# One PSUM ring of four banks in place of two pairs, and attention ahead of the weights in the prologue

## The chip, the cores and the metric

One core of one Trainium2 chip runs the program. The metric is device time in microseconds (us). Three timed runs of the kernel before took 955.02 to 955.73 us, median 955.3.

## The reference

```python
scores = (q @ k.T) / sqrt(64)                  # 4 batches, 8 heads, 576 positions, head size 64
# heads 0-3: window of 32 positions; heads 4-7: 32 positions with dilation 4
attn = softmax(where(mask, scores, -1e9)); x = attn @ v        # -> 2304 tokens x 512
h = x @ w_in;  x = (s * relu(h)**2 + b) @ w_out                # 512 -> 2048 -> 512
h = x @ w_in2; out = (h * cos(h)) @ w_out2                     # 512 -> 2048 -> 512
```

## The kernel before

The tokens are cut into five tiles of 384, 384, 512, 512 and 512 columns (tiles 0 to 4). For both MLPs (m = 0, 1) and each tile there are 16 steps, one per slice of 128 hidden rows. Step p of the program multiplies slice p into a PSUM tile `h` (`mm_in`), and multiplies the activated slice of two steps earlier into four PSUM tiles `y` (`mm_out`). From tile 1 on each product is three fp32r matmuls (high and low parts); tile 0 of the first MLP uses plain fp32 matmuls.

Attention is cut into units: 192 positions of a pair of heads. A unit is a matmul for the scores (`a_scores`, tile `sc`), a softmax on VectorE (mask and scale into `sm`, maximum) and ScalarE (the exponentials, three or four instructions), a normalisation on VectorE (`a_norm`), a transpose on TensorE (`a_transpose`, tile `tp`) with a copy into `pt`, a product with v (`a_pv`, tile `pv`) and a copy into the input `xy` of the MLP. Units 0 to 7 make tile 0 and run in the prologue, k = 0 to 11: iteration k issues scores of unit k, normalisation of unit k-1, transpose of unit k-3 and pv of unit k-4. The later units run beside the first MLP, one tile of tokens ahead: a unit whose scores stand in step p has its softmax at the end of p, its normalisation at the head of p+1, its transpose at the end of p+2 and its pv in p+4. In steps 15 to 26 and 31 to 42 there is a unit in every step; they are called dense here. A softmax buffer `sm` is one of two, so the softmax of a unit waits until the transpose of the unit before last has read its buffer.

The weights come as 64-bit words, 32 halves of 128x512 per MLP (half 2f feeds `mm_in` of slice f, half 2f+1 feeds `mm_out`). A half is loaded on SP's queue (`w_load`, 512 KB), opened by two ScalarE instructions (`w_float`) and joined by four VectorE instructions (`w_join`); `w_whole(n)` joins up to half n and opens one half further. `W_FIRST` says behind which attention loads the first four halves are loaded, `W_STEPS` after which prologue iterations how many halves are joined, and `w_point` joins up to half 2p + WPRE (rounded with the half step) in step p of tile 0.

Engines take their instructions in the order in which they are written; the schedule is by hand. PSUM has eight banks: four for y, two for h (`ps_h`), two for sc, tp and pv (`ps_a`). A pool hands out its banks in turn, so in a pool of two a tile waits until the tile before last has been read. In the second MLP h alternates between the two pools.

Of the kernel before, what the change touches and what calls it, by code (L numbers as in the profile page):

```python
# [28 lines left out]
NCC = DM // P  # L29
NFC = DFF // P  # L30
LAG = (2, 3)
W_FIRST, W_STEPS = (3, 5, 6, 7), {5: 1, 7: 2, 8: 3, 9: 4, 10: 5, 11: 6}
V_LATE = 3
AHEAD = 3
WPRE, W_PACE = 7, 2.0
IN_CUT = 13

BG = (0, 4, 8, 10, 10)
# [14 lines left out]
def attention_then_two_mlps(ctx, tc, qk_p, qk_d, v_p, v_d, mask_p, mask_d, w1, w2, sv, bv, out):  # L53
    nc = tc.nc
    pool = lambda name, bufs, **kw: ctx.enter_context(tc.tile_pool(name=name, bufs=bufs, **kw))
    PSUM = bass.MemoryType.PSUM
# [4 lines left out]
    xspool = pool("xs", 4)  # L61
    gpool = pool("g", 1)
    ps_y = pool("ps_y", 1, space=PSUM)
    ps_h = pool("ps_h", 2, space=PSUM)
    ps_a = pool("ps_a", 2, space=PSUM)

    s_sb = const.tile([P, 1], F32, tag="s_sb", name="s_sb")
    b_sb = const.tile([P, 1], F32, tag="b_sb", name="b_sb")
# [107 lines left out]
    def a_load_first(i, what):  # L176
        tb, hp = units[i]
        b, u = divmod(tb, 3)
        dil = hp >= 2
        nb, nq, nk = (4, DB, DK) if dil else (3, PB, PK)  # L180
        kw = nb * nk if dil else 3 * PB + WINDOW
        d = st.setdefault(i, dict(dil=dil, nb=nb, nq=nq, nk=nk, tb=tb, hp=hp, b=b, u=u))
        place = lambda n, shape: wpool.tile(
            shape, F32, tag=("wh", "wl")[(5 * i + n) % 2] + str(2 * NFC - 1 - (5 * i + n) // 2), name=f"first{n}_{i}"
        )
        d["place"] = place
        if what == "v":
            d["v"] = place(2, [nk, nb, P])
            nc.sync.dma_start(d["v"], (v_d if dil else v_p)[b, hp % 2, u])
        else:  # L190
            src = (qk_d if dil else qk_p)[b, hp % 2, u]
            d["q"], d["k"] = place(0, [P, 384]), place(1, [P, kw])
            nc.sync.dma_start(d["q"], src[:, :384])
            nc.sync.dma_start(d["k"], src[:, 384:])
# [60 lines left out]
    def a_norm(i):  # L255
        d = st[i]
        nb, nq, nk = d["nb"], d["nq"], d["nk"]
        nr = 2 * nq
        rec = ap_.tile([nr, nb, 1], F32, tag="rec", name=f"rec{i}")
        nc.vector.tensor_scalar_add(d["ssum"], d["ssum"], 1e-9)  # L260
        nc.vector.reciprocal(out=rec[:, :, 0], in_=d["ssum"])
        nc.vector.tensor_tensor(out=d["sm"], in0=d["sm"], in1=rec.to_broadcast([nr, nb, nk]), op=ALU.mult)

    def a_transpose(i, ps, copy=None):
        d = st[i]
        nb, nq, nk = d["nb"], d["nq"], d["nk"]
        nr = 2 * nq
        acc = ps.tile([P, 512], F32, tag=ps_tag[ps.name], name=f"tp{i}")
        for j in range(nb):
            nc.tensor.transpose(acc[:nk, j * nr : (j + 1) * nr], d["sm"][:, j, :], ident[:nr, :nr])  # L270
        pt = d["place"](4, [nk, 384]) if "place" in d else ap_.tile([nk, 384], F32, tag="pt", name=f"pt{i}")
        (copy or nc.vector.tensor_copy)(pt, acc[:nk, :384])
        d["pt"] = pt
# [25 lines left out]
                src = acc[:, lo:hi]  # L299
            nc.scalar.copy(dst, src)  # L300

    ps_tag = {ps_y.name: "y0", ps_h.name: "h", ps_a.name: "a"}


    xs = {}
# [12 lines left out]
    def mm_in(m, t, fc, ps):  # L318
        h = ps.tile([P, 512], F32, tag=ps_tag[ps.name], name=f"h{m}_{t}_{fc}")
        hps[m, t, fc] = h  # L320
        for cc in range(NCC):
            cs = slice(cc * P, (cc + 1) * P)
            if m == 0 and t == 0:
                w = w32[m, 2 * fc].bitcast(F32)
                nc.tensor.matmul(  # L325
                    h[:, : SIZES[t]], w[:, cs], xy[t][:, cc, :], start=cc == 0, stop=cc == NCC - 1
                )
                continue
            x = xs[m, t, cc]
            hi, lo = wh[m, 2 * fc][:, cs], wl[m, 2 * fc][:, cs]  # L330
            nc.tensor.matmul(h[:, : SIZES[t]], hi, x[:, 0, :], start=cc == 0, stop=False)  # L331
            nc.tensor.matmul(h[:, : SIZES[t]], hi, x[:, 1, :], start=False, stop=False)  # L332
            nc.tensor.matmul(h[:, : SIZES[t]], lo, x[:, 0, :], start=False, stop=cc == NCC - 1)  # L333
# [96 lines left out]
    with tc.manual_schedule():  # L430
# [4 lines left out]
        def w_load_to(n):  # L435
            while wq[0] < min(n, 2 * NFC):
                w_load(0, wq[0], stage.tile([P, DM], I64, tag=f"s{wq[0] % 5}", name=f"stage{wq[0]}"))
                wq[0] += 1
# [18 lines left out]
        for i in range(1, n0 + V_LATE):  # L457
            if i < n0:
                a_load_first(i, "qk")
            if 0 <= i - V_LATE < n0:  # L460
                a_load_first(i - V_LATE, "v")
            if i == 3:
                nc.sync.dma_start(m_d, mask_d.rearrange("p (j k) -> p j k", j=2))
            if i == 5:
                nc.sync.dma_start(s_sb, sv.to_broadcast([P, 1]))
                nc.sync.dma_start(b_sb, bv.to_broadcast([P, 1]))
            if i in W_FIRST:
                w_load_to(wq[0] + 1)
        a_load(n0)
        a_load(n0 + 1)  # L470
        for k in range(n0 + 4):
            if k < n0:
                a_scores(k, ps_a)
                a_softmax(k)
            if 0 <= k - 1 < n0:
                a_norm(k - 1)
            if 0 <= k - 3 < n0:
                a_transpose(k - 3, ps_h, nc.scalar.copy if k % 2 else None)
            if 0 <= k - 4 < n0:
                a_pv(k - 4, ps_y, f"y{k % NCC}")  # L480
            if k in W_STEPS:
                w_whole(W_STEPS[k])
# [7 lines left out]
        for i in range(n0, len(units)):  # L490
            t = next(t for t in range(NTILE) if i < first_unit[t + 1])
            n, j = first_unit[t + 1] - first_unit[t], i - first_unit[t]
            p = (t - 1) * NFC + ((0, 1, 3, 4, 6, 8, 9, 10)[j] if n == 8 else j - 1)
            at((p, 0), lambda i=i: a_scores(i, ps_a))
            at((p + 1, 1), lambda i=i: a_load_v(i))
            if i + 2 < len(units):
                at((p, 0), lambda i=i: a_load(i + 2))
            at((p, 1), lambda i=i: a_softmax(i))
            at((p + 1, 0), lambda i=i: a_norm(i))
            at((p + 2, 2), lambda i=i: a_transpose(i, ps_a, nc.scalar.copy))  # L500
            at((p + 4, 0), lambda i=i: a_pv(i, ps_a))
# [16 lines left out]
        k = 0  # L518
        for t, n in enumerate(BG):
            for i in range(n):  # L520
                b = t * NFC + (2 if t == 1 else 0) + (i + 0.5) * (NFC - (2 if t == 1 else 0)) / n
                p, ph = int(b), 1 + int(b % 1 >= 0.5)
# [17 lines left out]
        for p in range(NP + LAG[1]):  # L540
            if p < NP:
                m, t, fc = where(p)
                mm_in(m, t, fc, ps_h if (m == 0 or fc % 2 == 0) else ps_a)
                nxt = p - fc + NFC
                if nxt < NP:
                    mm, tt, _ = where(nxt)
                    for cc in {NFC - 1: range(NCC)}.get(fc, ()):
                        x_split(mm, tt, cc)
            fire(p, 0)
            if p < NP and m == 1:  # L550
                cos1(t, fc)
            if NTILE * NFC <= p - 1 < NP:
                cos_split(*where(p - 1)[1:])
            po = p - LAG[0] if p < NTILE * NFC + LAG[0] else p - LAG[1]
            out_now = po >= 0 and p != NTILE * NFC + LAG[0]
            last = out_now and where(po)[2] == NFC - 1
            if last:
                mm_out(*where(po))
                y_out(*where(po)[:2])
            if p < NP:  # L560
                w_point(p, 0)
                if m == 0:
                    relu2(t, fc)
                else:
                    cos2(t, fc)
                    cos3(t, fc)
            if out_now and not last:
                mm_out(*where(po))
            if p < NFC * NTILE:
                w_point(p, 1)  # L570
            f = p - NFC * (NTILE - 1)
            if 0 <= f < NFC:
                w_fetch(2 * f)
            if 0 <= f - LAG[0] < NFC:
                w_fetch(2 * (f - LAG[0]) + 1)
            fire(p, 1)
            fire(p, 2)
            if p == NFC:
                assert wq[2] == 2 * NFC
                stage_scope.close()  # L580
                late.append(ctx.enter_context(tc.tile_pool(name="late", bufs=1, side="right", reuse_waits="tile")))
            if p == NFC * (NTILE - 1) - 1:
                att.close()
                after_att.append(ctx.enter_context(tc.tile_pool(name="after_att", bufs=1)))
                for t in (0, 1):
                    xy[t] = after_att[0].tile([P, NCC, SIZES[t]], F32, tag=f"xy{t}", name=f"back{t}")
                    nc.sync.dma_start(xy[t], parked[t])
# [88 lines left out]
```

## Time and profile before

| | us |
|---|---|
| median of three runs | 955.3 |
| profiled execution, its own time | 957.32 |
| its span, first to last instruction | 955.3 |
| TensorE busy with matmuls | 915.1 (96%) |
| VectorE busy | 589.4 (62%) |
| ScalarE busy | 504.7 (53%) |

In the timelines each row gives start, duration, engine, line and operation, output and inputs by name, and in brackets how long the engine idled before it and who released it.

### The profile page before, as it was taken

To read this page: it belongs to the slowest core of one execution; us is meant where nothing else is said; L and a number is where in the kernel's file an instruction comes from. 1 tells how busy PE (TensorE), PEld (TensorE's weight loads), DVE (VectorE), ACT (ScalarE), POOL (GpSimd) and SP (SyncE) were. 2 spreads that over 40 slices of the span, in tenths; PEclk is the share of its full clock that TensorE was granted. 3 is DMA by queue.
4 is the path that set the end of the run, shared out by engine and by line. 5 is a ranking of instruction groups with operands and counts; after the bars stand their busy time and mean duration, and the time that the engine had idled before them with its cause. 6 is when DMAs were issued, how large, how long until landed. Compare 5 with 4: busy or idle time off the path is not lost.

```text
span 955.3 us, 13248 instructions
## 1 busy us (share of the span) xinstructions
PE 915.1 (96%) x4888; PEld 764.3 (80%) x4888; DVE 589.4 (62%) x1156; ACT 504.7 (53%) x1166; POOL 0.7 (0%) x6
## 2 busy tenths in 40 slices
PE   6779998889989999999999999999999999999998
PEld 6545667779967778888888899999988888888886
DVE  4978756665655547654754676666665665566554
ACT  5666655556645546554643564554554454454443
POOL 0000000000000000000000000000000000000000
PEclk9989999999999999999999999999999999999999
DMA  8656503332434334443689940000000000001001
GB/s 251 211 190 226 187 21 117 98 108 101 131 99 153 107 116 152 151 141 102 243 292 302 310 153 1 1 34 1 1 34 0 1 22 23 1 1 44 1 1 44
DMA packets 45535, 99.62 MB, mean 104 GB/s; under 512 B 5440, under 2 KB 12064, under 8 KB 45472
## 3 DMA queue, kind: packets, MB, share of 16 engines
q1 hardware_dynamic: 45472, 98.80, 31.3%
q8 instruction: 38, 0.62, 0.3%
q14 instruction: 25, 0.20, 0.1%
HBM read 75.71 MB, written 23.07 MB: 103 GB/s over the span
## 4 chain that ended last, share of the span: by engine, by line
PE 84%; DVE 8%; ACT 6%; issue 1%; DMA 1%; SPq 1%; ACTq 0%; DVEq 0%
PE y L348 13%; PE y L349 12%; PE y L350 12%; PE h L331 11%; PE h L333 11%; PE h L332 11%; PE y L345 4%; PE sc L219 3%; PE h L325 3%; ACT sm L249 3%; PE pv L282 2%; PE tp L270 1%; DVE wa L132 1%; DVE nmax L246 1%; DVE wa L129 1%; DVE sm L237 1%
## 5 line engine op out<-in xcount | busy, mean ns | idle before, releaser
L348 PE MATMUL y<-g,wh 128*128 128x512 f32 (+1 forms) x576 | 219.7, 381 | 0.0
L331 PE MATMUL h<-xs,wh 128*128 128x512 f32 (+1 forms) x576 | 217.3, 377 | 0.0
L350 PE MATMUL y<-g,wl 128*128 128x512 f32 (+1 forms) x576 | 216.0, 375 | 0.0
L349 PE MATMUL y<-g,wh 128*128 128x512 f32 (+1 forms) x576 | 215.8, 375 | 0.0
L333 PE MATMUL h<-xs,wl 128*128 128x512 f32 (+1 forms) x576 | 214.1, 372 | 0.0
L332 PE MATMUL h<-xs,wh 128*128 128x512 f32 (+1 forms) x576 | 213.9, 371 | 0.0
L350 PEld LDWEIGHTS y<-g,wl 128*128 128x128 f32 x576 | 109.5, 190 | 15.5
L348 PEld LDWEIGHTS y<-g,wh 128*128 128x128 f32 x576 | 109.5, 190 | 15.1
L349 PEld LDWEIGHTS y<-g,wh 128*128 128x128 f32 x576 | 109.6, 190 | 14.4
L333 PEld LDWEIGHTS h<-xs,wl 128*128 128x128 f32 x576 | 108.1, 188 | 15.4
L332 PEld LDWEIGHTS h<-xs,wh 128*128 128x128 f32 x576 | 108.3, 188 | 14.8
L331 PEld LDWEIGHTS h<-xs,wh 128*128 128x128 f32 x576 | 108.1, 188 | 14.6
L249 ACT ACTIVATE sm<-sm,nmax 96x80 f32<-96x80 f32 (+1 forms) x140 | 49.8, 356 | 113.2 <-DVE nmax L246 113.2
L415 ACT ACTIVATE n<-n 128x512 f32<-128x512 f32 (+1 forms) x80 | 47.2, 590 | 102.2 <-DVE n L409 102.1
L405 ACT ACTIVATE n<-h,pmagic 128x512 f32<-128x512 f32 (+1 forms) x80 | 51.7, 646 | 87.2 <-PE h L333 86.3
L406 DVE TENSOR_SCALAR n<-n 128x512 f32<-128x512 f32 (+1 forms) x80 | 32.0, 400 | 87.0 <-ACT n L405 87.0
L421 DVE SCALAR_TENSOR_TENSOR n<-n,h 128x512 f32<-128x512 f32 (+1 forms) x80 | 50.6, 633 | 55.2 <-ACT n L416 55.2
L389 ACT ACTIVATE r<-h 128x512 f32<-128x512 f32 (+1 forms) x80 | 44.5, 556 | 31.8 <-PE h L333 25.9
L399 DVE CAST g<-r 128x512 fp32r<-128x512 f32 (+1 forms) x64 | 26.1, 407 | 50.7 <-ACT r L397 50.6
L123 DVE TENSOR_SCALAR wa<-wa 128x512 f32<-128x512 f32 x62 | 26.2, 422 | 48.6 <-ACT wa L116 43.2
L409 DVE SCALAR_TENSOR_TENSOR n<-n,r 128x512 f32<-128x512 f32 (+1 forms) x80 | 51.1, 638 | 2.8
L408 DVE SCALAR_TENSOR_TENSOR r<-n,h 128x512 f32<-128x512 f32 (+1 forms) x80 | 50.7, 634 | 2.8
(82 smaller groups left out, 1094.7 us busy)
## 6 DMA issues: line engine op xcount, KB each, us to landing
stage<-w SPq DMA_DIRECT2D x32, 512.0 KB, 4.0
raw<-w SPq DMA_DIRECT2D x32, 512.0 KB, 4.8
cut<-raw SPq DMA_DIRECT2D x32, 256.0 KB, 2.3
cut<-wa SPq DMA_DIRECT2D x32, 256.0 KB, 2.6
wh<-cut SPq DMA_DIRECT2D x32, 256.0 KB, 3.7
wl<-cut SPq DMA_DIRECT2D x32, 256.0 KB, 4.2
qk<-qk_d SPq DMA_DIRECT2D x20, 352.0 KB, 3.0
qk<-qk_p SPq DMA_DIRECT2D x20, 304.0 KB, 3.0
```

What stands on the lines that cost most here:

```text
L249: nc.scalar.activation(out=sm[:, j, :], in_=sm[:, j, :], func=AF.Exp, bias=nmax[:, j : j + 1], scale=1.0, accum_out=ssum[:, j : j + 1],)
L331: nc.tensor.matmul(h[:, : SIZES[t]], hi, x[:, 0, :], start=cc == 0, stop=False)
L332: nc.tensor.matmul(h[:, : SIZES[t]], hi, x[:, 1, :], start=False, stop=False)
L333: nc.tensor.matmul(h[:, : SIZES[t]], lo, x[:, 0, :], start=False, stop=cc == NCC - 1)
L348: nc.tensor.matmul(y[:, : SIZES[t]], hi, g[:, 0, :], start=fc == 0, stop=False)
L349: nc.tensor.matmul(y[:, : SIZES[t]], hi, g[:, 1, :], start=False, stop=False)
L350: nc.tensor.matmul(y[:, : SIZES[t]], lo, g[:, 0, :], start=False, stop=fc == NFC - 1)
L405: nc.scalar.activation(out=n, in_=h[:, : SIZES[t]], func=AF.Identity, scale=1.0 / TWO_PI, bias=pmagic)
L408: nc.vector.scalar_tensor_tensor(out=r, in0=n, scalar=-C1, in1=h[:, : SIZES[t]], op0=ALU.mult, op1=ALU.add)
L409: nc.vector.scalar_tensor_tensor(out=n, in0=n, scalar=-C2, in1=r, op0=ALU.mult, op1=ALU.add)
L415: nc.scalar.activation(out=r, in_=r, func=AF.Sin, scale=0.5)
L421: nc.vector.scalar_tensor_tensor(out=r, in0=r, scalar=-1.0, in1=h[:, : SIZES[t]], op0=ALU.add, op1=ALU.mult)
```

## The change

The two pools of two banks become one pool of four, `ps_a`, for h, sc, tp and pv alike. In the prologue the first four weight halves are loaded behind the attention data of units 4 to 7, three halves are joined there instead of six, all copies of transposes run on VectorE (before, units 0, 2, 4 and 6 had ScalarE), and s and b are loaded later. In tile 0 of the MLP the halves run 4 ahead of the step's pace instead of 7, and the eight units of tile 1 stand in steps 3 to 10 instead of 0, 1, 3, 4, 6, 8, 9, 10. The line numbers after line 62 fall by one.

```diff
-W_FIRST, W_STEPS = (3, 5, 6, 7), {5: 1, 7: 2, 8: 3, 9: 4, 10: 5, 11: 6}
+W_FIRST, W_STEPS = (7, 8, 9, 10), {8: 1, 9: 2, 11: 3}
-WPRE, W_PACE = 7, 2.0
+WPRE, W_PACE = 4, 2.0
-    ps_h = pool("ps_h", 2, space=PSUM)
-    ps_a = pool("ps_a", 2, space=PSUM)
+    ps_a = pool("ps_a", 4, space=PSUM)
-            if i == 5:
+            if i == 10:
                 nc.sync.dma_start(s_sb, sv.to_broadcast([P, 1]))
-                a_transpose(k - 3, ps_h, nc.scalar.copy if k % 2 else None)
+                a_transpose(k - 3, ps_a)
-            p = (t - 1) * NFC + ((0, 1, 3, 4, 6, 8, 9, 10)[j] if n == 8 else j - 1)
+            p = (t - 1) * NFC + (((3, 4, 5, 6, 7, 8, 9, 10) if t == 1 else (0, 1, 3, 4, 6, 8, 9, 10))[j] if n == 8 else j - 1)
-                mm_in(m, t, fc, ps_h if (m == 0 or fc % 2 == 0) else ps_a)
+                mm_in(m, t, fc, ps_a)
```

VectorE at the end of the prologue, before (`first3_6` is the softmax of unit 6, `first4_n` the copied transpose of unit n, `wa0_n` half n):

```order
L262 TENSOR_TENSOR first3_6_325<-first3_6_325,rec6_366 96x320
L123 TENSOR_SCALAR wa0_1_311<-wa0_1_311 128x512
L126 TENSOR_SCALAR wa0_1_311<-wa0_1_311 128x512
L129 SCALAR_TENSOR_TENSOR wa0_1_311<-stage1_149,wa0_1_311 128x512
L132 ISA wa0_1_311<-stage1_149,wa0_1_311 128x1024
L260 TENSOR_SCALAR ssum7_361<-ssum7_361 96x4
...
L272 COPY first4_5_403<-tp5_398 80x384
L123 TENSOR_SCALAR wa0_2_385<-wa0_2_385 128x512
```

The same place in the changed kernel:

```order
L271 COPY first4_5_379<-tp5_374 80x384
L122 TENSOR_SCALAR wa0_0_391<-wa0_0_391 128x512
L125 TENSOR_SCALAR wa0_0_391<-wa0_0_391 128x512
L128 SCALAR_TENSOR_TENSOR wa0_0_391<-stage0_154,wa0_0_391 128x512
L131 ISA wa0_0_391<-stage0_154,wa0_0_391 128x1024
L271 COPY first4_6_408<-tp6_403 80x384
...
L271 COPY first4_7_434<-tp7_429 80x384
L122 TENSOR_SCALAR wa0_2_420<-wa0_2_420 128x512
```

Half 0 has moved behind the last softmax; halves 0 and 1 now stand ahead of the copies of units 6 and 7.

TensorE with its waits in the dense steps 19 and 20 (tile 1), before (sc20 and sc21 are the scores issued in steps 19 and 20):

```order
L219 MATMUL sc20_1461<-qk20_1318 128x96 [waits DMAHW1_49,PE_49,Activation_49]
...
L270 MATMUL tp18_1503<-ident_95,sm18_1350 96x128 [waits Activation_49]
...
L331 MATMUL h0_1_4_1516<-xs0_1_0_1205,wh0_8_1334 128x384
...
L282 MATMUL pv17_1529<-pt17_1431,v17_1348 64x64 [waits DMAHW3_49,DVE_49]
...
L219 MATMUL sc21_1541<-qk21_1385 128x96 [waits DMAHW4_49,PE_49,Activation_49]
```

The same place in the changed kernel:

```order
L218 MATMUL sc20_1458<-qk20_1315 128x96 [waits DMAHW1_49,DVE_49]
...
L269 MATMUL tp18_1500<-ident_92,sm18_1347 96x128 [waits PE_49,Activation_49]
...
L330 MATMUL h0_1_4_1513<-xs0_1_0_1202,wh0_8_1331 128x384 [waits Activation_49]
...
L281 MATMUL pv17_1526<-pt17_1428,v17_1345 64x64 [waits DMAHW3_49,Activation_49]
...
L218 MATMUL sc21_1538<-qk21_1382 128x96 [waits DMAHW4_49,DVE_49]
```

The order is the same; the waits have changed places: sc waits for VectorE in place of ScalarE, pv for ScalarE in place of VectorE, and h has a wait for ScalarE that it had not.

## Rows read from the trace of the kernel before

**Rows 1.** The page: part 1, first line, and part 2, the clock.

```profile
PE 915.1 (96%) x4888; PEld 764.3 (80%) x4888; DVE 589.4 (62%) x1156; ACT 504.7 (53%) x1166; POOL 0.7 (0%) x6
...
PEclk9989999999999999999999999999999999999999
```

**Rows 2.** Waits of TensorE, 0 to 128 us: for whom, total, times, longest.

```profile
PE pv L282 <- DVE first L272: 4.6, 3, 2.3
...
PE pv L282 <- DVE sm L237: 3.9, 1, 3.9
```

**Rows 3.** Timeline of TensorE, prologue and tile 0.

```profile
13.74 1.54 PE L219 MATMUL sc<-first,first 128*96 128x80 f32 x8 [2.90 <-DMA first<-qk_d]
...
22.70 1.54 PE L219 MATMUL sc<-first,first 128*96 128x80 f32 x8
...
38.20 5.17 PE L325 MATMUL h<-xy,wa 128*128 128x384 f32 x8
...
47.10 2.77 PE L325 MATMUL h<-xy,wa 128*128 128x384 f32 x8
...
108.89 0.91 PE L219 MATMUL sc<-qk 128*96 128x80 f32 x8
...
141.95 0.64 PE L331 MATMUL h<-xs,wh 128*128 128x384 f32 x1
```

**Rows 4.** Timeline of VectorE, prologue and tile 0.

```profile
36.58 0.55 DVE L272 COPY first<-tp 80x384 f32<-80x384 f32 x1
...
57.03 0.42 DVE L123 TENSOR_SCALAR wa<-wa 128x512 f32<-128x512 f32 x1
...
66.35 0.45 DVE L237 SCALAR_TENSOR_TENSOR sm<-sc,m_p 128x288 f32<-128x288 f32 x1
...
73.94 0.45 DVE L237 SCALAR_TENSOR_TENSOR sm<-sc,m_p 128x288 f32<-128x288 f32 x1
```

**Rows 5.** Waits of TensorE, 128 to 240 us.

```profile
PE sc L219 <- ACT pt L272: 8.1, 7, 1.7
PE sc L219 <- DVE sm L237: 1.6, 1, 1.6
```

**Rows 6.** Waits of TensorE, 240 to 340 us.

```profile
PE sc L219 <- ACT pt L272: 5.9, 7, 2.1
```

**Rows 7.** Windows: busy of PE, PEld, DVE, ACT, POOL; then granted clock, DMA share, GB/s.

```profile
160.00:170.00 10.00, 8.35 (x52) 7.77 (x51) 6.06 (x14) 4.81 (x15) 0.00 (x0) 0.83 0.33 110
...
270.00:290.00 20.00, 19.39 (x110) 15.62 (x111) 10.54 (x25) 8.95 (x28) 0.00 (x0) 0.91 0.41 130
```

**Rows 8.** Timeline of VectorE, tile 1: softmax starts of steps 17, 19, 22, 23, 25.

```profile
156.59 0.45 DVE L237 SCALAR_TENSOR_TENSOR sm<-sc,m_p 128x288 f32<-128x288 f32 x1
...
169.72 0.46 DVE L237 SCALAR_TENSOR_TENSOR sm<-sc,m_p 128x288 f32<-128x288 f32 x1 [1.74 <-PE tp L270]
...
191.16 0.49 DVE L237 SCALAR_TENSOR_TENSOR sm<-sc,m_d 96x320 f32<-96x320 f32 x1 [0.21 <-PE tp L270]
...
197.59 0.49 DVE L237 SCALAR_TENSOR_TENSOR sm<-sc,m_d 96x320 f32<-96x320 f32 x1 [0.22 <-PE tp L270]
...
214.47 0.49 DVE L237 SCALAR_TENSOR_TENSOR sm<-sc,m_d 96x320 f32<-96x320 f32 x1 [1.66 <-PE tp L270]
```

**Rows 9.** Timeline of ScalarE, step 20: relu reads h.

```profile
174.06 0.48 ACT L389 ACTIVATE r<-h 128x384 f32<-128x384 f32 x1
```

**Rows 10.** Timeline of TensorE, tile 1: scores of steps 22 and 23, transpose of step 26.

```profile
187.74 0.91 PE L219 MATMUL sc<-qk 128*96 128x80 f32 x8 [0.98 <-ACT pt L272]
...
194.16 0.90 PE L219 MATMUL sc<-qk 128*96 128x80 f32 x8 [0.45 <-ACT pt L272]
...
220.34 0.49 PE L270 MATMUL tp<-ident,sm 96*80 96x96 f32 x4
```

**Rows 11.** Timeline of VectorE, tile 2: two softmax starts.

```profile
283.55 0.46 DVE L237 SCALAR_TENSOR_TENSOR sm<-sc,m_p 128x288 f32<-128x288 f32 x1 [0.74 <-PE tp L270]
...
290.76 0.49 DVE L237 SCALAR_TENSOR_TENSOR sm<-sc,m_d 96x320 f32<-96x320 f32 x1 [1.20 <-PE tp L270]
```

More of the change, by code (lines that the diff above doesn't have):

```diff
@@ L300, in a_pv @@
             nc.scalar.copy(dst, src)
-    ps_tag = {ps_y.name: "y0", ps_h.name: "h", ps_a.name: "a"}
+    ps_tag = {ps_y.name: "y0", ps_a.name: "a"}
     xs = {}
```

## The prediction

> **What bounds the kernel now.** I read the page first: TensorE is busy 96% of the span [rows 1], so a gain can come only from the 40 us in which it is not (955.3 - 915.1) and from stretches at half clock. The waits of TensorE by stretch then say where these lie. In the prologue and tile 0 the longest are for VectorE's copies of transposes, 4.6 us, and one of 3.9 us of a pv for the softmax of another unit [rows 2]. In tile 1 the scores wait seven times for ScalarE's copy `pt`, 8.1 us together, and once for a softmax, 1.6 us [rows 5]; in tile 2 again seven times, 5.9 us [rows 6]. From tile 3 on, and in the second MLP, I found no such wait before the last few microseconds, and h has a ring of four banks there already, so I count these parts at nothing. So there are three terms: prologue with tile 0, tile 1, tile 2. The sum is made on the profiled execution; its span, 955.3 us, equals the median of the runs, so differences go straight onto the median.
>
> **Prologue and tile 0.** Before, TensorE starts h of step 0 at 38.20 us [rows 3]. It stands behind pv of unit 7, and that behind VectorE's copy at 36.58 [rows 4], ahead of which four halves are joined. Now two halves stand ahead of it. One half costs 2.33 us of VectorE: four of them fill 57.03 to 66.35 [rows 4]. That is 4.7 us earlier. Two copies that were ScalarE's now stand in VectorE's queue behind the softmax of unit 7, 0.55 us each [rows 4], some 1.0 us later. The 512 KB of half 0 no longer lie ahead of unit 4's data, for which the scores wait 2.90 us at 13.74 [rows 3]. What that saves lies between 0 and 2.9; other loads are in flight together, so I take 1.2. From there TensorE goes on at its own pace to unit 7 (8.96 us for three units, 13.74 to 22.70 [rows 3]). The copy starts at 36.58 - 4.7 + 1.0 - 1.2 = 31.7, and h of step 0 about 33.3.
>
> From there VectorE sets the pace, not TensorE. It ends half 2 at 34.5 (31.7, the copy of 0.5 and 2.33) and has eight halves (3 to 10) to join before the first softmax, of unit 8 in step 3: 18.6 us. I add 0.8 us, because ScalarE opens half 5 only behind the relu of step 0, and that h takes 5.17 us where the next ones take 2.77 [rows 3]. So this softmax starts at 53.9. In steps 4 to 10 each holds two halves and a unit: 7.59 us (66.35 to 73.94 [rows 4]). The softmax of step 9 starts at 53.9 + 6 x 7.59 = 99.4; the scores of step 10 wait for the bank that it reads, and start at 99.9. TensorE alone would be there at about 95 (18 products of h and y at 2.7, one at 5.17, some 8 us of units), so it keeps up. Before, the last scores start at 108.89 and the first h of tile 1 at 141.95 [rows 3], with TensorE busy throughout; now one more pv, 0.6 us, lies in between. **Gain 108.89 - 99.9 - 0.6 = 8.4 us.** Bounds: 4 (loads save nothing, and ScalarE is late for two more halves) and 11 (all of the 2.9 and 1 us of VectorE hidden).
>
> [...]
>
> **Tile 1.** In a dense step four banks are handed out: h, pv, sc, tp. In a ring of four each then takes the bank of its own kind of the step before. The scores of step p wait for the softmax read of p-1 (VectorE), no longer for a copy that ScalarE makes behind the exponentials of that softmax; pv waits for the copy of the last pv, long done; and h waits for the relu of p-1, which is new. So the 8.1 us of waits for `pt` go. What is late next is the chain from softmax to softmax on VectorE and ScalarE, through exponentials, normalisation, splits of weights, and a half of the second MLP in steps 19 and 23. Between step 17 and step 25 it took 214.47 - 156.59 = 57.88 us, of which 1.74 + 0.21 + 0.22 + 1.66 = 3.83 were waits for TensorE [rows 8]: 54.05 us, or 6.76 a step, where TensorE needs 194.16 - 187.74 - 0.45 = 5.97 [rows 10]. So the softmax of step 25 comes at 156.59 + 54.05 = 210.6 on the old clock. The relu of a step ends 4.8 us behind the softmax before it (174.06 + 0.48 - 169.72 [rows 8, 9]); so relu of step 26 ends, and h of step 27 may start, at 215.4, against 220.6 before, behind the transpose at 220.34 [rows 10]. **Gain 5.2 us.** Behind the waiting h stand pv, scores and y on TensorE, and ScalarE and VectorE wait for those in turn; this loop is in the number. Bounds: 0, if each wait is only renamed, and 11.4, if all 9.7 us of waits go [rows 5] and with them a half-clock stretch (0.83 granted over 10 us, 1.7 us [rows 7]).
>
> **Tile 2.** Here VectorE waits for TensorE before the softmax, 0.74 and 1.20 us [rows 11], though half of the steps hold a half to join; so the chain has room and TensorE is free to run. The 5.9 us go [rows 6], and most of the half-clock stretch (0.91 over 20 us, 1.8 us [rows 7]; I take 1.5). **Gain 7.4 us.** Bounds 4.5 and 7.7. In tiles 3 and 4 nothing waits; a ring that h shares costs nothing there as long as relu is read within a step, as in tile 2.
>
> **Sum.** 955.3 - 8.4 - 5.2 - 7.4 = **934.3 us**. s and b loaded later cost nothing: they are first used at the end of tile 0.
>
> **The rivals.**
> - *The halves come late (0.15).* With three halves ahead, TensorE waits for halves 4, 6 and 8, each wait delays relu, and relu delays the opening of the next half. By the sum half 4 is joined at 39.2 and wanted at about 41, so 2 us of lateness would start it. Then tile 0 gains 1.5 instead of 8.4: 941.2.
> - *The ring clears tile 1 wholly (0.13).* If VectorE makes up time in steps without a half: 955.3 - 8.4 - 11.4 - 7.4 = 928.1. Against it: 6.76 against 5.97 us.
> - *The ring only renames the waits (0.08).* Only tile 0 gains: 946.9. Against it: the copy that is waited for now comes behind the exponentials, the softmax read ahead of them. [...]
> - *The clock still falls (0.07).* Waits of about 1 us remain in tile 1 behind each half, and rows of 0.83 and 0.91 stand beside waits of that length now [rows 5 to 7]. Then 1.7 and 1.5 us come back: 937.5. [...]
> - *Slower (0.03): h hangs on ScalarE.* h now waits for the relu one step back, and ScalarE takes relu behind exponentials, copies and the opening of halves. Two steps then take the time to relu, 4.8, and a step of TensorE, 5.97: 10.8, less than two chain links. That turns round once relu is 3.7 us later (2 x 7.24 is a pair of links now, 57.88 / 8 each [rows 8]). At 5 us later a step takes 7.9, 0.66 more, in 22 dense steps 14.5: 955.3 - 8.4 + 14.5 = 961.4.
> - *No change (0.02):* the gains of tile 0 are eaten by such waits.
>
> **How the numbers follow.** The forecast has 0.52. What can be told from no change here is about 0.2%, 1.9 us. Faster: 0.52 + 0.15 + 0.13 + 0.08 + 0.07 = 0.95; same 0.02; slower 0.03. The range 926 to 943 takes in the forecast with its bounds, the late halves, the cleared tile 1 and the falling clock, and leaves out the renamed waits and the slower case.
>
> **What would show it.** Right: h of step 0 near 33 us, the first h of tile 1 near 133.5, no waits of scores for `pt` in tiles 1 and 2, some short waits of h for relu and of scores for a softmax behind steps 19 and 23, and none in tile 2. Wrong: waits of h in tile 0 for a half, or of h for relu in every dense step.

## The result and the profile after

The changed kernel takes 933.39 us (median of four runs, 932.4 to 934.58), the kernel before beside it 955.16 us (954.84 to 955.73): 21.8 us less, ratio 0.9772 with a 95% interval of 0.9755 to 0.9789. Forecast: 934.3.

The profiled executions differ by 22.9 us in their spans (955.3 and 932.4). That is 1.1 us more than the medians do: the profiled execution of the kernel before took 957.32 us, 2.2 above its median, that of the changed kernel 934.18, 0.8 above. The page after, TensorE's line and the granted clock by slices (before: [rows 1]):

```profile
PE 906.8 (97%) x4888; PEld 758.3 (81%) x4888; DVE 590.2 (63%) x1160; ACT 503.0 (54%) x1162; POOL 0.7 (0%) x6
...
PEclk9799999999999999999999999999999999999999
```

TensorE does the same work in 8.3 us less busy time and idles 14.6 us less (932.4 - 906.8 = 25.6, before 40.2). The waits of TensorE after, from 0 to 133 us, and from 133 to 225 us (the columns are engine, line, what it waited for, us together, times, the longest); from 225 to 330 us there are none:

```profile
PE pv L281 <- DVE first L271: 4.9, 6, 1.4
PE sc L218 <- DMA first<-qk_p: 4.3, 2, 3.6
PE sc L218 <- DVE sm L236: 3.4, 3, 2.2
PE pv L281 <- issue: 2.2, 1, 2.2
PE h L324 <- ACT pt L271: 1.9, 2, 1.6
...
PE sc L218 <- DVE sm L236: 4.2, 3, 2.1
PE h L330 <- ACT pt L271: 0.6, 1, 0.6
```

No scores wait for `pt` any more: 8.1 us and seven waits in tile 1 [rows 5], 5.9 us and seven waits in tile 2 [rows 6] are gone. In tile 1 three waits of scores for a softmax stand in their place. The wait of 3.9 us of a pv for a softmax [rows 2] is gone too; in tile 0 the scores now wait three times for a softmax, 3.4 us, and h twice for ScalarE's copy `pt`, 1.9 us, which the forecast did not have.

That h waits for `pt` at all comes from the order in which the ring is handed out. In the first and last steps of a run of units not all four kinds of tile are under way, so h does not take the bank of the last h: by the order of the program, h of steps 7 and 12 (tile 0), 19 (tile 1) and 35 (tile 2) takes a bank that a transpose had, and needs its copy. Steps 7, 12 and 19 are the three waits above; the copy that step 19 waits for ends at 150.34 us, its h starts at 150.40, and the next relu only at 150.77.

Where the 22.9 us lie is read from three starts in TensorE's timeline: h of step 0, the first h of tile 1, the first h of tile 2. Of the kernel after:

```profile
31.13 9.88 PE L324 MATMUL h<-xy,wa 128*128 128x384 f32 x24
...
133.12 0.64 PE L330 MATMUL h<-xs,wh 128*128 128x384 f32 x1
...
231.71 0.39 PE L330 MATMUL h<-xs,wh 128*128 128x512 f32 x1
```

The first two marks of the kernel before are in [rows 3]; its first h of tile 2:

```profile
246.25 0.39 PE L331 MATMUL h<-xs,wh 128*128 128x512 f32 x1
```

So the prologue is 38.20 - 31.13 = 7.07 us shorter, tile 0 is 103.75 - 101.99 = 1.76 shorter, tile 1 is 104.30 - 98.59 = 5.71 shorter, and all from tile 2 on 709.05 - 700.69 = 8.36 shorter.

The forecast for these stretches was 4.9, 3.5, 5.2 and 7.4. The time came within 1 us of the forecast; the shares of the prologue and of tile 0 did not, and that their errors nearly cancel is luck.

### The profile page after: what moved, and what is told of

It is laid out like the page before. It is cut to its first block, busy times and chain, and to the rows that moved or that the text cites. A ratio compares the mean times of both kernels' runs of the same rounds, so it can differ in the third digit from the quotient of the medians.

```text
span 932.4 us, 13282 instructions
## 1 busy us (share of the span) xinstructions
PE 906.8 (97%) x4888; PEld 758.3 (81%) x4888; DVE 590.2 (63%) x1160; ACT 503.0 (54%) x1162; POOL 0.7 (0%) x6
## 4 chain that ended last, share of the span: by engine, by line
PE 83%; DVE 10%; ACT 5%; issue 1%; DMA 0%; SPq 0%; DVEq 0%; ACTq 0%
PE y L347 13%; PE y L349 12%; PE y L348 12%; PE h L330 12%; PE h L332 12%; PE h L331 12%; PE sc L218 2%; ACT sm L248 2%; PE pv L281 2%; PE h L324 2%; PE y L344 2%; DVE wa L131 1%; DVE wa L128 1%; DVE nmax L245 1%; PE tp L269 1%
## 5 line engine op out<-in xcount | busy, mean ns | idle before, releaser
L349 PEld LDWEIGHTS y<-g,wl 128*128 128x128 f32 x576 | 108.7, 189 | 15.3
L332 PEld LDWEIGHTS h<-xs,wl 128*128 128x128 f32 x576 | 108.1, 188 | 15.3
```

Of the source, the lines that this page charges most:

```text
L349: nc.tensor.matmul(y[:, : SIZES[t]], lo, g[:, 0, :], start=False, stop=fc == NFC - 1)
```

## The experiments

Eleven kernels ran, each beside the kernel before on the same chip (955.58, 954.35 or 955.64 us there). The table has them all. The columns after the time are lengths of stretches in the profiled execution, by the marks above: start to h of step 0, tile 0, tile 1, and tile 2 to the end. Each row is one execution, and spans are read to 0.1 us, so the second decimal of the last column says nothing.

| kernel | median us | prologue | tile 0 | tile 1 | from tile 2 |
|---|---|---|---|---|---|
| before | 955.16 | 38.20 | 103.75 | 104.30 | 709.05 |
| changed | 933.39 | 31.13 | 101.99 | 98.59 | 700.69 |
| ring alone | 938.89 | 36.98 | 101.11 | 97.83 | 700.68 |
| order alone | 946.85 | 31.01 | 103.95 | 102.79 | 707.45 |
| loads early | 937.79 | 35.01 | 101.82 | 97.85 | 700.72 |
| copies on ScalarE | 933.19 | 31.46 | 101.74 | 97.83 | 700.67 |
| halves 7 ahead | 941.06 | 36.41 | 103.82 | 98.13 | 700.64 |
| halves 3 ahead | 935.42 | 28.66 | 105.70 | 98.53 | 700.71 |
| halves 2 ahead | 949.18 | 30.70 | 117.26 | 97.86 | 700.68 |
| units in old steps | 932.12 | 31.13 | 100.67 | 97.84 | 700.66 |
| halves in light steps | 930.49 | 30.61 | 101.52 | 91.69 | 704.68 |
| two halves to tile 2 | 928.91 | 32.33 | 100.24 | 91.68 | 703.65 |
| halves a step earlier | 926.00 | 30.90 | 100.69 | 91.64 | 700.87 |

### Ring alone, order alone

Ring alone is the kernel before with the pool changed and nothing else; order alone is the changed kernel with the two pairs put back.

```diff
-    ps_h = pool("ps_h", 2, space=PSUM)
-    ps_a = pool("ps_a", 2, space=PSUM)
+    ps_a = pool("ps_a", 4, space=PSUM)
-                a_transpose(k - 3, ps_h, nc.scalar.copy if k % 2 else None)
+                a_transpose(k - 3, ps_a, nc.scalar.copy if k % 2 else None)
-                mm_in(m, t, fc, ps_h if (m == 0 or fc % 2 == 0) else ps_a)
+                mm_in(m, t, fc, ps_a)
```

> The kernel before with the one ring of four banks alone (prologue, halves ahead and units as before). Theory (three separate terms): tiles 1 and 2 gain 5.7 + 8.3 = 14.0 us, the prologue and tile 0 nothing: about 941, no scores waiting for pt, h of step 0 still at about 38 us. Rival (the ring only renames the waits): 953 to 956, waits of h for relu or of scores for softmax in most dense steps. Rival (the ring helps tile 0 as well): below 938.

Measured: 938.89 us, ratio 0.9824 (0.98 to 0.9848).

```diff
-    ps_a = pool("ps_a", 4, space=PSUM)
+    ps_h = pool("ps_h", 2, space=PSUM)
+    ps_a = pool("ps_a", 2, space=PSUM)
-                a_transpose(k - 3, ps_a)
+                a_transpose(k - 3, ps_h)
-                mm_in(m, t, fc, ps_a)
+                mm_in(m, t, fc, ps_h if (m == 0 or fc % 2 == 0) else ps_a)
```

> The changed kernel with the two pairs of banks put back; prologue, halves ahead, loads and units as changed. Theory (separate terms): the gain of the prologue and tile 0 stays, 8.8 us, and the scores wait for pt in tiles 1 and 2 as before: about 946.3, first h of tile 1 near 133. Rival (tile 0 needs the ring too, because units in steps 3 to 10 hand out banks densely): 950 or more, first h of tile 1 at 137 or later.

Measured: 946.85 us, ratio 0.9907 (0.9876 to 0.9938). Its waits of TensorE from 133 to 225 us are those of the kernel before to the tenth [rows 5]:

```profile
PE sc L219 <- ACT pt L272: 8.1, 7, 1.7
PE sc L219 <- DVE sm L237: 1.6, 1, 1.6
PE pv L282 <- DVE sm L237: 0.8, 1, 0.8
```

It has waits in tile 0 that neither the kernel before nor the changed one has to that extent. From 0 to 133 us:

```profile
PE sc L219 <- ACT pt L272: 4.8, 4, 1.6
```

(before: one of 1.2 us; changed: none). Of ring alone, the stretch from 133 to 225 us:

```profile
PE sc L218 <- DVE sm L236: 5.4, 6, 2.0
PE h L330 <- ACT pt L271: 0.6, 1, 0.6
PE tp L269 <- ACT pt L271: 0.5, 1, 0.5
```

The ring gives all that tile 1 and tile 2 gain, and of tile 0 besides, which I had not put down to it: 103.75 to 101.11, with 4.5 us of waits there instead of 6.3 and one of two half-clock windows gone (granted 0.84 and 0.82 from 60 to 80 us before, 0.83 from 60 to 70 now). Half clock is what the profile grants in such a stretch: 0.50 from 67 to 71 us before, where the six matmuls of a unit's scores take 1.59 us (at 68.92) and not 0.80 (at 43.21, granted 1.00). The order gives the gain of the prologue, but by itself nothing in tile 0 (103.95 against 103.75): there the units in steps 3 to 10 make the pairs of banks wait. So the rival of order alone held in part; its first h of tile 1 came at 134.96, between 133 and 137. The 1.2 us that ring alone shows in the prologue lie in the wait of unit 4's scores for data, 1.71 us instead of 2.90, and its edit moves no load; I take them for scatter between executions. The 1.5 and 1.6 us of order alone in tile 1 and from tile 2 on stand beside unchanged waits: there the trace has one half-clock stretch fewer in each, so the same waits can come with such a stretch or without (before, granted 0.83 from 160 to 170, from 210 to 220 and from 270 to 280 us; order alone, 0.96 and 0.87 from 193 to 213 us, and 1.00 in all windows from 240 to 310). Together the parts gain 16.7 + 8.7 = 25.4 us by medians, the change 21.8; they overlap by 3.6. The rival "the ring only renames the waits" is out. Ring alone adds no bank, it lets all kinds of tile share the four there were, and gave 16.7 us; no run here has more banks.

### What the prologue gains from

Three runs undo one part of the order each. First the loads:

```diff
-W_FIRST, W_STEPS = (7, 8, 9, 10), {8: 1, 9: 2, 11: 3}
+W_FIRST, W_STEPS = (3, 5, 6, 7), {8: 1, 9: 2, 11: 3}
-            if i == 10:
+            if i == 5:
```

> The changed kernel with the first four loads of weights and those of s and b back among the loads of attention data. Theory as forecast: the scores of unit 4 wait again, up to 2.9 us, of which 1.2 us reach h of step 0 (32.3 us): 934 to 935. [...] Rival (the copies on VectorE hide the loads): 932 to 934, h of step 0 at 31.1.

Measured: 937.79 us, ratio 0.9832 (0.9814 to 0.9851), h of step 0 at 35.01, 3.88 us later: both lie above the theory's numbers. TensorE's timeline of this run, the scores of units 4 to 7:

```profile
12.77 1.54 PE L218 MATMUL sc<-first,first 128*96 128x80 f32 x8 [1.84 <-DMA first<-qk_d]
...
15.72 1.57 PE L218 MATMUL sc<-first,first 128*96 128x80 f32 x8
...
18.70 1.57 PE L218 MATMUL sc<-first,first 128*96 128x80 f32 x8
...
21.68 1.57 PE L218 MATMUL sc<-first,first 128*96 128x80 f32 x8
```

and of the changed kernel, units 4, 6 and 7:

```profile
10.73 0.98 PE L218 MATMUL sc<-first,first 128*96 128x80 f32 x8
...
15.67 0.90 PE L218 MATMUL sc<-first,first 128*96 128x80 f32 x8
...
17.86 0.91 PE L218 MATMUL sc<-first,first 128*96 128x80 f32 x8
```

The same eight matmuls take 1.57 us there and 0.90 here. The granted clock is 1.00 in both kernels from 10 to 20 us, but scores of this shape take 1.51 us at 167.97 in the changed kernel, where it is 0.50; so I read 1.57 as half clock too, and go by the durations. A unit takes 18.70 - 15.72 = 2.98 us there and 17.86 - 15.67 = 2.19 here. So the loads cost twice: unit 4 starts 2.04 us later (12.77 against 10.73), and at the lower level behind it unit 7 starts 3.82 us later (21.68 against 17.86).

Then the copies:

```diff
-                a_transpose(k - 3, ps_a)
+                a_transpose(k - 3, ps_a, nc.scalar.copy if k % 2 else None)
```

> The changed kernel with the copies of every second transpose of the prologue back on ScalarE. Theory as forecast: two copies of 0.5 us leave VectorE's queue ahead of the copy of unit 7 and of h, h of step 0 at 30.1, time 931.5 to 933. Rival (ScalarE makes these copies behind the exponentials of the unit just before, so that pv waits for them): h of step 0 at 31 to 33, time 933.5 to 936.

Measured: 933.19 us against 933.39, h of step 0 at 31.46 against 31.13. Neither the theory's time nor the rival's came. The copies cost nothing on VectorE; the 1.0 us of the sum isn't there. The waits only change their name, here from 0 to 133 us:

```profile
PE pv L281 <- ACT first L271: 4.4, 3, 1.9
...
PE pv L281 <- DVE first L271: 2.4, 2, 2.1
```

Then the halves ahead:

```diff
-W_FIRST, W_STEPS = (7, 8, 9, 10), {8: 1, 9: 2, 11: 3}
+W_FIRST, W_STEPS = (7, 8, 9, 10), {5: 1, 7: 2, 8: 3, 9: 4, 10: 5, 11: 6}
-WPRE, W_PACE = 4, 2.0
+WPRE, W_PACE = 7, 2.0
```

> The changed kernel with the halves ahead as before (four ahead of the copy of unit 7, seven ahead of tile 0's steps), ring, loads and units as changed. Theory (halves on VectorE at 2.33 us each set the prologue and tile 0): h of step 0 two halves later, at 31.1 + 4.7 = 35.8 us, the last softmax of tile 0 three halves later, first h of tile 1 at 133.1 + 7.0 = 140.1, time 939 to 941. Rival (TensorE sets tile 0, so only the prologue counts): first h of tile 1 at 137.8 or earlier, 936 to 938.5. Rival (halves ahead are no loss, since tile 0 then waits less): 932 to 935.

Measured: 941.06 us, ratio 0.9862 (0.9847 to 0.9877); h of step 0 at 36.41 (+5.28), the first h of tile 1 at 140.23 (+7.11, expected 7.0). A pv of this run waits 4.9 us for VectorE's copy, behind the halves:

```profile
PE pv L281 <- DVE first L271: 9.1, 7, 4.9
```

The halves are the larger part of what the order gains. Undone one at a time, loads and halves cost 3.88 + 5.28 = 9.2 us of the prologue, while order and ring together gain 7.07: each hides a part of the other. In tile 0 the three further halves cost 1.83 us (103.82 against 101.99).

### Fewer halves ahead

```diff
-W_FIRST, W_STEPS = (7, 8, 9, 10), {8: 1, 9: 2, 11: 3}
+W_FIRST, W_STEPS = (7, 8, 9, 10), {8: 1, 11: 2}
-WPRE, W_PACE = 4, 2.0
+WPRE, W_PACE = 3, 2.0
```

> The changed kernel with one half fewer (one ahead of the copy of unit 7, three ahead of tile 0's steps). Theory (each half is 2.33 us of VectorE ahead of the last softmax of tile 0, as three more halves cost 7.1 us): first h of tile 1 at 130.8, time 930.5 to 931.5. Rival (the edge on which halves come late lies here already, as with two fewer, where h waited 20 us for halves in 12 steps): waits of h for wa in several steps, first h of tile 1 at 135 or later, time 935 to 945.

Measured: 935.42 us, ratio 0.9786 (0.9766 to 0.9805), an interval that overlaps the changed kernel's. With two ahead (`{11: 1}`, `WPRE = 2`):

> The changed kernel with two halves fewer still (one in the prologue, behind the copy of unit 7; two ahead of tile 0's steps). Theory (the number of halves ahead sets tile 0 and TensorE has room): h of step 0 near 28 us, first h of tile 1 at 133.1 - 4.7 = 128.5, time 928 to 930. Rival (halves come late: TensorE waits for halves in steps 1 to 4, relu comes late and so does the opening of the next): waits of h or y for wa of over 5 us together, half clock behind them, time 933 to 940.

Measured: 949.18 us, ratio 0.9947 (0.9931 to 0.9964). The waits of h for halves in the two runs, three ahead and then two:

```profile
PE h L324 <- DVE wa L131: 6.0, 6, 1.2
```
```profile
PE h L324 <- DVE wa L131: 17.6, 11, 4.1
...
PE h L324 <- DVE last_two L131: 2.4, 1, 2.4
```

and TensorE's timeline of the run with two, steps 0 to 2 and the last two of tile 0:

```profile
30.70 7.97 PE L324 MATMUL h<-xy,wa 128*128 128x384 f32 x16 [3.52 <-DVE wa L131]
42.75 4.49 PE L324 MATMUL h<-xy,wa 128*128 128x384 f32 x8 [4.07 <-DVE wa L131]
...
132.05 2.82 PE L324 MATMUL h<-xy,wa 128*128 128x384 f32 x8 [2.39 <-DVE wa L131]
140.65 4.44 PE L324 MATMUL h<-xy,last_two 128*128 128x384 f32 x8 [2.39 <-DVE last_two L131]
```

(The run with two was made first.) By the traces the edge lies just below four. One half fewer brings h of step 0 forward by 2.5 us and loses 3.7 in tile 0. Two fewer lose 15.3 in tile 0: the last steps have no unit, and take 140.65 - 132.05 = 8.6 us each, which I read as the loop from h over relu, the opening and the joining back to h. Both theories missed here, and of the run with two the rival's time as well (933 to 940); what came is the rivals' mechanism. VectorE's work ahead of the softmaxes does not set tile 0 alone; below four halves, when a half arrives does.

### Units of tile 1 in the old steps

```diff
-            p = (t - 1) * NFC + (((3, 4, 5, 6, 7, 8, 9, 10) if t == 1 else (0, 1, 3, 4, 6, 8, 9, 10))[j] if n == 8 else j - 1)
+            p = (t - 1) * NFC + ((0, 1, 3, 4, 6, 8, 9, 10)[j] if n == 8 else j - 1)
```

> The changed kernel with the units of tile 1 back in steps 0, 1, 3, 4, 6, 8, 9, 10 instead of 3 to 10. Theory (VectorE sets the pace up to the softmax of step 9, and the work ahead of it is the same in both orders): first h of tile 1 within 1.5 us of 133.1, time 932 to 935, though TensorE waits in other steps. Rival (a softmax in steps 0 and 1 holds up the joining, and h and y wait for halves, with half clock behind each wait): 936 to 942.

Measured: 932.12 us; ratio 0.9749 (0.9729 to 0.9769), an interval that overlaps the changed kernel's. The first h of tile 1 stands at 131.80, 1.3 us earlier in this one trace. This part of the change brings nothing that these runs show; that it costs a microsecond is not shown, since two of the four runs of the changed kernel took 932.4 and 932.61 us.

### The halves in tile 1

Four halves of the second MLP are opened in tile 1, two of them between softmaxes of dense steps (19 and 23). Two rows of VectorE and one of TensorE from the timeline of the changed kernel:

```profile
159.07 0.45 DVE L236 SCALAR_TENSOR_TENSOR sm<-sc,m_p 128x288 f32<-128x288 f32 x1
167.46 0.45 DVE L236 SCALAR_TENSOR_TENSOR sm<-sc,m_p 128x288 f32<-128x288 f32 x1
...
167.97 1.51 PE L218 MATMUL sc<-qk 128*96 128x80 f32 x8 [2.06 <-DVE sm L236]
```

From one softmax to the next it takes 8.39 us across the half of step 19, where 153.31 to 159.07 took 5.76 (in the six steps without a half from 147.77 to 201.49 it is 5.5 to 6.7); the scores then wait 2.06 us, and their 1.51 us for eight (0.91 at 98.72) stand at the head of a half-clock stretch, granted 0.50 from 168.3 to 171 us. The same comes behind step 23 (a wait of 1.56 us, 1.52 us for eight at 195.29, granted 0.51 from 195.3 to 198.7). So I moved the halves behind the units:

```diff
-                b = t * NFC + (2 if t == 1 else 0) + (i + 0.5) * (NFC - (2 if t == 1 else 0)) / n
+                b = t * NFC + (11 if t == 1 else 0) + (i + 0.5) * (NFC - (11 if t == 1 else 0)) / n
```

> The changed kernel with the four halves of the second MLP that are opened in tile 1 (steps 19, 23, 26, 30) moved behind the units, to steps 27 to 31. Theory (a half in a dense step makes the next softmax late, and the scores wait for it): the waits of 2.06 and 1.56 us at 168 and 195 us go, and the half clock behind them, (1 - 0.90) x 10 + (1 - 0.93) x 10 + (1 - 0.83) x 10 = 3.4 us: 926.4 to 929.8. Rival (splits of weights and exponentials set the chain, not the halves): 932 to 935, waits elsewhere in tile 1. Rival (closer together, the halves make the end of tile 1 late): above 935.

Measured: 930.49 us, ratio 0.9729 (0.9711 to 0.9748). Tile 1 shrinks by 6.90 us, to 91.69, as expected; but tile 2 gives 4.0 back, and the time misses the 926.4 to 929.8. There the one wait from 225 to 330 us stands, and the granted clock of the window behind it is 0.83 (columns: window, length, PE busy, PEld, DVE, ACT, POOL, clock, DMA share, GB/s):

```profile
244.05 0.50 PE L330 MATMUL h<-xs,wh 128*128 128x512 f32 x1 [2.13 <-ACT pt L271]
...
240.00:250.00 10.00, 7.87 (x41) 5.82 (x41) 5.55 (x13) 5.54 (x19) 0.00 (x0) 0.83 0.48 174
```

ScalarE's timeline of that stretch shows why h waits: exponentials, the opening of a half, which waits for its load, and only then the copy `pt`.

```profile
240.87 0.38 ACT L248 ACTIVATE sm<-sm,nmax 128x96 f32<-128x96 f32 x1 [2.41 <-DVE nmax L245]
...
242.42 0.66 ACT L115 ACTIVATE wa<-raw 128x512 f32<-128x512 f32 x1 [0.36 <-DMA raw<-w]
242.99 0.65 ACT L116 ACTIVATE raw<-raw 128x512 int32<-128x512 uint32 x1
243.55 0.45 ACT L271 COPY pt<-tp 96x384 f32<-96x384 f32 x1
243.91 0.59 ACT L388 ACTIVATE r<-h 128x512 f32<-128x512 f32 x1
```

This h (step 35) waits for the copy `pt` and not for a relu: the copy ends at 244.00, h starts at 244.05, and the relu beside it ends only at 244.50. It costs 2.13 us of wait and 1.7 of half clock (0.17 of 10 us). The opening alone does not explain it: in the changed kernel a half is opened ahead of the same copy, and h does not wait. The slower rival's mechanism, h behind a late relu, shows in none of the traces; every wait of h for ScalarE over 0.25 us ends with a copy (`pt`, or pv into `xy`) or, once, with the opening of a half. Two runs try to be rid of the wait of step 35, both with the units of tile 1 in the old steps. The first moves two halves into tile 2 (`BG = (0, 2, 10, 10, 10)`, the two left behind the units):

> The changed kernel with the units of tile 1 in the old steps, and of the second MLP's halves only two in tile 1 (behind its units), ten in tile 2. Theory (a half in a dense step of tile 1 is what its chain can't take; tile 2 has room): first h of tile 1 at 131.8, tile 1 in 91.7 us as without halves in dense steps, tile 2 as changed: 932.1 - 6.1 = 926. Rival (in tile 2 the two further halves make softmaxes late there, or h waits for relu behind a late load): tile 2 longer by 3 us or more, time 929 to 932.

Measured: 928.91 us, ratio 0.9715 (0.9691 to 0.9738). Tile 1 is 91.68 again, but h waits 1.5 us, again for the copy `pt`, and 0.5 for a split near the start of tile 2, and the rest is 3.0 us longer: the rival in its size, 0.1 us below its range of times. The second keeps four in tile 1, the last of them one step earlier:

```diff
-                b = t * NFC + (2 if t == 1 else 0) + (i + 0.5) * (NFC - (2 if t == 1 else 0)) / n
+                b = (26.5, 27.75, 29.0, 30.25)[i] if t == 1 else t * NFC + (i + 0.5) * NFC / n
```

> The changed kernel with the units of tile 1 in the old steps and the four halves of tile 1 at 26.5, 27.75, 29.0 and 30.25 steps (before 19.75, 23.25, 26.75, 30.25; in the run with light steps the last stood at 31.4). Theory (the wait of h for relu at 244 us came from a half whose load stood on SP behind the writing out of a half of the step before; with the last half a step earlier it goes): tile 1 in 91.7 us and no wait in tile 2, about 926. Rival (it is the number of halves next to each other, not the last one's place): a wait of h of some 2 us near the start of tile 2 and half clock behind it, about 930.

Measured: 926.00 us (925.46 to 927.87), ratio 0.9691 (0.967 to 0.9713), the time that the theory had: 7.4 us faster than the change. Tile 1 takes 91.64 us, tile 2 has no wait, and tile 1 has these two left:

```profile
PE h L330 <- ACT pt L271: 0.6, 1, 0.6
PE sc L218 <- DVE sm L236: 0.6, 1, 0.6
```

That the late load on SP was the cause is not shown, and the trace of the run with light steps speaks against it as the main part: ScalarE idled 0.36 us there for the load. The exponentials ahead of it were already late, waiting for VectorE. They start 240.87 - 223.82 = 17.05 us behind the first h of tile 2, in the last run 238.21 - 223.23 = 14.98. In between VectorE joins the last half of tile 1 (from 229.31 to 231.75 us), and the last run moves that joining a step earlier as well as the load. No run moved one of them alone.

## Why the prediction was right, and where it was not

**Prologue: right in sign, the load term too small.** The step that failed is "From there TensorE goes on at its own pace to unit 7 (8.96 us for three units)". The scores of unit 4 come at 10.73 and those of unit 7 at 17.86: 7.13 us, because TensorE reaches its faster level there (0.91 us for the eight matmuls of unit 7 instead of 1.54). The term of the loads, 1.2 us with an upper end of 2.9, measures 3.88 when undone alone, beyond its bound: I had priced the wait, not the slower matmuls behind it. The halves, 4.7 in the sum, measure 5.28; the copies, 1.0, measure nothing. Together the copy of unit 7 starts at 29.46 and not at 31.7:

```profile
29.46 0.55 DVE L271 COPY first<-tp 80x384 f32<-80x384 f32 x1
...
51.69 0.45 DVE L236 SCALAR_TENSOR_TENSOR sm<-sc,m_p 128x288 f32<-128x288 f32 x1
59.27 0.45 DVE L236 SCALAR_TENSOR_TENSOR sm<-sc,m_p 128x288 f32<-128x288 f32 x1
...
90.15 0.48 DVE L236 SCALAR_TENSOR_TENSOR sm<-sc,m_d 96x320 f32<-96x320 f32 x1
98.19 0.48 DVE L236 SCALAR_TENSOR_TENSOR sm<-sc,m_d 96x320 f32<-96x320 f32 x1
```

**Tile 0: the chain held, one cadence was short.** From that copy to the first softmax the forecast had 53.9 - 31.7 = 22.2 us; it is 22.23. The cadence of 7.59 us is 7.58 for the first units; but the later ones, of the dilated heads (mask `m_d`), take 98.19 - 90.15 = 8.04; they have four blocks instead of three, and VectorE waits 1.6 us for their exponentials instead of 1.3. "In steps 4 to 10 each holds two halves and a unit: 7.59 us" took the row of one kind of unit for both. From the scores of step 10, which wait for the softmax as forecast, to the first h of tile 1 it took 133.12 - 98.72 = 34.4 us, 0.8 more than the forecast's 33.6:

```profile
98.72 0.91 PE L218 MATMUL sc<-qk 128*96 128x80 f32 x8 [1.06 <-DVE sm L236]
```

So the lead of 2.2 us shrank, and the first h of tile 1 came at 133.12 for 133.5: errors of opposite sign, and luck. That the gain of tile 0 belongs to the order alone was wrong as well: order alone left tile 0 at 103.95, ring alone brought it to 101.11, and the halves count there (1.83 us) with the ring in place.

**Tile 1: right.** The chain of softmaxes from step 17 to step 25 took 201.49 - 147.77 = 53.72 us for 54.05, and the stretch gained 5.71 for 5.2. The surplus of the chain over TensorE, 6.76 against 5.97, comes down to the halves of steps 19 and 23: without them the tile loses all waits but two of 0.6 us. "In a ring of four each then takes the bank of its own kind of the step before" holds only once all four kinds are under way; one of those two waits, of h for `pt` in step 19, comes from the steps before that.

**Tile 2: right, a little small.** 8.36 for 7.4. The waits were 5.9 + 0.2 and the half clock 1.8 (granted 0.91 over 20 us [rows 7]), together 7.9; some 0.5 us I can't place. Order alone had the same waits, no half-clock stretch there (granted 1.00) and 1.6 us less than before (707.45 against 709.05), which fits that share; 6.76 us are left for the waits. So some 1.6 of the 8.36 us may belong to the one execution of the kernel before that was profiled.

**The sum.** "Its span, 955.3 us, equals the median of the runs, so differences go straight onto the median" was loose. The profiled execution took 957.32, 2.0 above that median. By spans the gain is 22.9, by medians 21.8.

**The rivals.** *Halves late* did not come; the 6.9 us that I gave for it lie between one half fewer, 2.0 us by the medians, and two fewer, 15.8: the price climbs far more steeply than I had it. *The ring clears tile 1* did not come by itself, but does without the halves in dense steps; the gain there is then 104.30 - 91.64 = 12.7, above my bound of 11.4. *Clock still falls* came in tile 1 and not in tile 2 (granted 1.00 in all windows from 230 to 300 us): windows of the changed kernel,

```profile
160.00:170.00 10.00, 7.94 (x56) 7.30 (x55) 5.82 (x14) 6.33 (x22) 0.00 (x0) 0.90 0.23 68
170.00:180.00 10.00, 10.00 (x69) 9.58 (x69) 7.07 (x17) 6.80 (x22) 0.00 (x0) 0.93 0.45 139
...
190.00:200.00 10.00, 8.33 (x58) 7.58 (x58) 7.47 (x17) 6.75 (x23) 0.00 (x0) 0.83 0.26 89
```

but it cost 0.7 us, not 1.7: the run with the units in the old steps, whose clock is 1.00 in all these windows (0.91 us for eight scores at 166.66 behind a wait of 2.05, and at 193.94 behind one of 1.58), takes 97.84 for tile 1 instead of 98.59. The chain of softmaxes sets the pace there, so TensorE can catch up. *h hangs on ScalarE* did not come by its mechanism: in no dense step did h wait for a relu. h waited for the copy `pt` instead, while the ring filled: 1.9 us in tile 0, 0.6 in tile 1, and 2.13 in tile 2 of the run with light steps.

## What to carry to other kernels

Where several kinds of tile share PSUM in a fixed order, ask which reader each kind waits for: one ring of four in place of two pairs moved the wait of the scores from the last instruction of a chain (`pt`) to its first (the softmax), and that was worth some 14 us here. Write down the first steps too, in which the ring is not yet in step: there h took the bank of a transpose, and a late copy on ScalarE held it up by as much as 2.13 us. Work that is dropped into a dense step shows as the next step's wait (2.06 us here); move it to steps in which the chain has slack. Price an idle spell of TensorE with the slower matmuls that can follow it, from rows at both levels (here 1.51 and 0.91 us for eight scores, each behind a wait of 2.1 us), and test the edge of a prefetch distance on both sides: here 7 and 2 were both worse than 4, by 8 and 16 us.

## What I had not expected of the hardware

In the prologue TensorE can reach its faster level at 10 to 17 us (0.90 us for the eight matmuls of a unit's scores, 1.57 at the lower one), long before the unbroken matmuls of h (from 31.13 us in the changed kernel). In ten of the thirteen traces the scores of unit 7 take 0.90 or 0.91 us for eight; there the scores of unit 4 had waited for their data by 0.67 us or less. In the other three they had waited 2.90 (before), 1.71 (ring alone) and 1.84 us (loads early), and all scores up to unit 7 take 1.54 to 1.57. Those three are the kernels that load the first weights among the attention data, and the ten are all those that load them later; loads early moves the loads alone. That the loads bring this about is so far shown; which idle time decides is not. The granted clock of the profile shows 1.00 from 0 to 20 us both in the kernel before and in the changed one, so it does not tell this level; durations of one shape do.

In the changed kernel the level was lost again at about 21 us, behind a wait of 1.16 us, and stayed low into the first h; here the granted clock shows it, 0.50 from 21.2 to 34.8 us:

```profile
21.74 1.09 PE L281 MATMUL pv<-first,first 80*64 80x48 f32 x16 [1.16 <-DVE first L271]
```

The same 16 matmuls take 0.67 at the higher level in tile 0. They take that too behind the same wait of 1.16 us in the run with three halves ahead, and 1.10 there only one unit later, behind a further wait of 0.57 us:

```profile
22.11 0.67 PE L281 MATMUL pv<-first,first 80*64 80x48 f32 x16 [1.16 <-DVE first L271]
```

So this wait does not by itself explain the loss, and what the waits ahead of h of step 0 still cost no run shows.
